# A GEGLU kernel whose head reads its weights on a second DMA queue and computes one tile, not two, the plain way

## The chip, the cores and the metric

The kernel runs on one core of one Trainium2 chip. The metric is the time of one execution in microseconds (us), measured on the device; the number that is quoted is the median of several runs. A profile's span is some 1.8 us shorter than the run's time (273.3 against 275.17 for the kernel before), so spans are compared with spans only.

PE is the matmul engine, DVE VectorE, ACT ScalarE, POOL GpSimd, SP SyncE. SP and ACT each have a DMA queue.

## The reference

```python
B, S, D, F = 32, 32, 1024, 3584        # 1024 tokens, all tensors bf16
def reference(x, w_gate, w_up, w_down):
    return (gelu(x @ w_gate) * (x @ w_up)) @ w_down   # tanh form of gelu
```

## The kernel before

The 3584 features are 28 tiles of 128. The tokens are two halves of 512, and so is the depth of 1024. A tile's gate and up results on both token halves are a 2 by 2 block product, which takes eight half products of four matmuls each. The kernel saves one of the eight with Strassen's scheme in Winograd's form: seven half products, of which P1 = a11·b11 and P2 = a12·b21 use the bf16 inputs as they are, and five use sums of weights (S1 to S4, by POOL) and of x (T1 to T4, by DVE) in fp32r. A tile is then 8 bf16 and 20 fp32r matmuls in place of 32 bf16 ones.

```python
def sums(ci, eng):                       # weights of chunk ci, two tiles each
    a11, a12, a21, a22 = quads(ci)       # gate upper, gate lower, up upper, up lower half of the depth
    yield eng.tensor_tensor(s1, a21, a22, ADD)
    yield eng.tensor_tensor(s2, s1, a11, SUB)
    yield eng.tensor_tensor(s4, a12, s2, SUB)
    yield eng.tensor_tensor(s3, a11, a21, SUB)
```

Sums need x whole and weights of both kinds, and at the start nothing has landed yet. So the head fills the time with work that needs little: tiles 0 and 1 are computed the plain way (32 matmuls each), and P2 of the next ten tiles, which needs only b21 (a quarter of x) and a12 (half of the gate weights), is computed ahead and kept in SBUF. Four tiles of these P2 are called a group here. Group 0's weights are the tile `a12a` (first buffer), group 1's the second buffer of `a12a`, group 2's `a12b`. x arrives as it lies in memory (`x_nat`, transposed by PE) for a first eighth, and by transposing DMAs (`load_xT`) for all else. This is the head's list of loads, in order of issue:

```python
load_nat(nc.sync, 0, 0, HALF)
load_nat(nc.scalar, 0, HALF, NB_P)
...
load_ahead(0, 0, 1)                       # group 0, first of four depth tiles
load_nat(nc.scalar, 1, 0, NB_P)
load_ahead(0, 1, 2, nc.scalar)
for which, eng in enumerate((nc.sync, nc.scalar)):
    load_w(eng, 0, which, KD, KD + KQ)
load_xT(0, KD + KQ, DT)                   # rest of b21, a transposing DMA
load_ahead(0, KQ, KD)                     # rest of group 0
load_w0(nc.sync, KD + KQ, DT)
load_ahead(1, 0, KD)                      # group 1
load_xT(0, 0, KD)                         # b11
load_w0(nc.sync, 0, KD)
load_xT(1, 0, KD)                         # b12
load_xT(1, KD, DT)                        # b22
```

And this is the order of PE's work in the head, with cuts:

```python
# half products of group 0 (depth tiles 0 and 1), as x_nat arrives
plain0(tok0, KD, KD + KQ)                 # tiles 0, 1, first token half
for j, copy in enumerate((nc.scalar.copy, nc.vector.tensor_copy) * 2):
    product_ahead(ps[j], 0, j, KQ)        # rest of group 0; needs the rest of b21
    copy(ahead[0][:, j, :], ps[j])
plain0(tok0, KD + KQ, DT)
...
for j, tag in enumerate("CCAA"):          # group 1
    ...
# tiles 0 and 1, rest of the first token half, then the second half
# P1 of chunk 1, P2 of group 2 (two tiles), then the loop over chunks, from S1·T1 on
```

## Time and profile before

| | before |
|---|---|
| median of 3 runs | 275.38 us (275.07 to 275.65) |
| span of the profiled run | 273.3 us |
| PE busy | 267.9 us, 98% |
| four bf16 matmuls of 512 columns, start to start | 0.86 us, 216 ns each |
| eight fp32r matmuls of 512 columns | 1.81 to 1.84 us, 227 ns each |
| first S1·T1 | 29.18 us |

The page of the kernel before gives, in its parts 1, 3 and 4, the engine's busy time, each DMA queue with its packets, MB and share of 16 engines (q1 is SP's, q10 is ACT's), and the shares of the chain of work that ended last.

```profile
span 273.3 us, 3350 instructions
PE 267.9 (98%) x1190; PEld 188.9 (69%) x1206; DVE 196.6 (72%) x196; ACT 110.8 (41%) x181; POOL 108.3 (40%) x55
...
q1 hardware_dynamic: 50304, 31.00, 39.3%
q10 hardware_dynamic: 3520, 2.56, 2.9%
...
PE 97%; DMA 1%; issue 0%; ACT 0%; SPq 0%
```

PE is nearly all of that chain: nothing else holds the time. SP's queue carries nearly everything. The timeline of PE before, in the head, lists start, length, engine, line, operation with its tiles, count, and in brackets idle time and what ended it. (Tile names come without their numbers: `b` is any quarter of x, `wg` and `wu` are gate and up weights, `t` and `s` the sums.)

```profile
4.45 0.61 PE L285 MATMUL psC<-b,a12a 128*128 128x256 bf16 x2 [0.54 <-DMA a12a<-in_w_gate_dram]
...
6.76 1.03 PE L252 MATMUL psA<-b,wg 128*128 128x512 bf16 x4
7.62 1.03 PE L252 MATMUL psB<-b,wu 128*128 128x512 bf16 x4
...
11.94 1.89 PE L285 MATMUL psC<-b,a12a 128*128 128x512 bf16 x8
13.66 1.89 PE L285 MATMUL psA<-b,a12a 128*128 128x512 bf16 x8
...
29.18 2.12 PE L270 MATMUL psC<-t,s 128*128 128x512 f32 x8
```

There is one piece of idle time, 0.54 us at 4.45 us. After that every start follows the one before by the matmuls' own time: 6.76 to 7.62 is four at 216 ns, 11.94 to 13.66 is eight (1.72 us). The Trainium skill, "TensorE: Matmul & The Clock Gate", Part 1, states about 215.7 ns, and this trace agrees. So there are two ways to a shorter time: fewer matmuls, or less idle head; and the second has little to give.

A table of stretches of the same head gives busy time per engine, granted clock, the share of DMA and, last, GB/s.

```profile
5.00:9.00 4.00, 4.00 (x30) 2.60 (x29) 0.49 (x2) 0.00 (x0) 0.00 (x0) 1.00 1.22 271
9.00:14.00 5.00, 4.95 (x24) 2.27 (x24) 1.52 (x3) 1.75 (x3) 0.00 (x0) 1.00 1.09 277
14.00:20.00 6.00, 6.00 (x30) 2.72 (x28) 3.85 (x4) 4.29 (x5) 0.00 (x0) 1.00 1.07 241
```

The DMA engines moved 271, 277 and 241 GB/s there. They were working all the time, and after 5 us PE never waited for them. Of the issues on SP's queue (start and length of the issuing instruction), these two: group 1's weights, and b11 by a transposing DMA.

```profile
5.44 0.47 SPq L204 DMA_DIRECT2D a12a<-in_w_gate_dram  x1
5.96 4.23 SPq L215 DMA_TRANSPOSE b<-in_x_dram  x1
```

Group 1's weights were issued at 5.44 us, ahead of the b11 transpose. They landed at 10.5 us and were needed at 11.94. The transpose then held SP's sequencer for 4.23 us, so whatever stands behind a transpose on this queue is issued late.

### The profile page before, as it was taken

What the parts mean: (1) busy time and instruction counts of PE and PEld (TensorE: products, weight loads), DVE (VectorE), ACT (ScalarE), POOL (GpSimd) and SP (SyncE); (2) the same over time, 40 slices, a digit from 0 to 9 for tenths busy, and PEclk for the clock granted to TensorE, in tenths of its full rate; (3) what the DMA queues carried; (4) which work ended last, traced back from release to release, by engine and by line L of the source; (5) the groups of instructions that cost most, each with busy time, mean ns of one, the idle gap of its engine ahead of it and who ended that gap; (6) DMA issues with size and microseconds to landing.
All of it is one profiled execution on the core that took longest, in us unless ns stands there. A gap on an engine that the chain in (4) does not pass through costs nothing.

```text
span 273.3 us, 3350 instructions
## 1 busy us (share of the span) xinstructions
PE 267.9 (98%) x1190; PEld 188.9 (69%) x1206; DVE 196.6 (72%) x196; ACT 110.8 (41%) x181; POOL 108.3 (40%) x55
## 2 busy tenths in 40 slices
PE   8999999999999999999999999999999999999995
PEld 4444777877778676676868686754447888888883
DVE  1269996877756676776667576568999999999611
ACT  1271664554643646455563636430300032972001
POOL 1000099997897694949576684000000000000000
PEclk9999999999999999999999999999999999999999
DMA  7994321414505405050514280004992254786202
GB/s 166 290 251 105 111 75 40 117 42 113 156 11 143 137 19 155 0 153 0 156 28 126 79 269 1 0 2 132 329 342 83 93 175 163 240 279 203 78 0 78
DMA packets 53841, 33.77 MB, mean 124 GB/s; under 512 B 9792, under 2 KB 53824, under 8 KB 53824
## 3 DMA queue, kind: packets, MB, share of 16 engines
q1 hardware_dynamic: 50304, 31.00, 39.3%
q10 hardware_dynamic: 3520, 2.56, 2.9%
q8 instruction: 9, 0.15, 0.3%
q14 instruction: 8, 0.07, 0.1%
HBM read 29.62 MB, written 2.10 MB: 116 GB/s over the span
## 4 chain that ended last, share of the span: by engine, by line
PE 97%; DMA 1%; issue 0%; ACT 0%; SPq 0%
PE psA L270 34%; PE psA L446 18%; PE psC L270 17%; PE psC L446 7%; PE psB L446 7%; PE psB L270 5%; PE psB L252 3%; PE psA L252 2%; PE psC L285 2%; PE psA L285 1%; DMA a12a<-in_w_gate_dram 1%; ACT o_sb L586 0%; SPq L191 0%; PE tp L243 0%
## 5 line engine op out<-in xcount | busy, mean ns | idle before, releaser
L270 PE MATMUL psA<-t,s 128*128 128x512 f32 x208 | 54.2, 402 | 0.0
L262 ACT ACTIVATE h<-c 128x512 bf16<-128x512 f32 x52 | 31.6, 627 | 36.6 <-DVE c L350 36.6
L270 PEld LDWEIGHTS psA<-t,s 128*128 128x128 f32 x208 | 39.1, 188 | 9.2
L168 POOL TENSOR_TENSOR s<-wu 128x1024 fp32r<-128x1024 bf16 x12 | 27.4, 2285 | 23.7 <-PE psC L270 12.8
L350 DVE TENSOR_TENSOR c<-sn,psA 128x512 f32<-128x512 f32 x26 | 17.8, 684 | 16.8 <-PE psA L270 16.8
L270 PEld LDWEIGHTS <-wg 128*128 128x128 bf16 x168 | 15.4, 98 | 20.1 <-issue 3.4
L169 POOL TENSOR_TENSOR s<-s,wg 128x1024 fp32r<-128x1024 f32 x12 | 27.7, 2312 | 0.9
L171 POOL TENSOR_TENSOR s<-wg,wu 128x1024 fp32r<-128x1024 bf16 x12 | 26.6, 2216 | 0.0
L355 ACT COPY sn<-psA 128x512 f32<-128x512 f32 x42 | 23.6, 584 | 6.8 <-PE psA L270 6.8
L355 ACT COPY sn<-psC 128x512 f32<-128x512 f32 x26 | 15.2, 588 | 26.9 <-PE psC L270 22.8
L270 PE MATMUL psA<-t,a22r 128*128 128x512 f32 x104 | 25.9, 391 | 0.0
L270 PE MATMUL psC<-t,s 128*128 128x512 f32 x104 | 25.8, 390 | 0.0
L270 PE MATMUL psC<-b22r,s 128*128 128x512 f32 x104 | 25.7, 389 | 0.0
L270 PE MATMUL psA<-b,wg 128*128 128x512 bf16 x100 | 24.1, 379 | 0.2
L270 PEld LDWEIGHTS psC<-t,s 128*128 128x128 f32 x104 | 19.4, 188 | 4.4 <-ACT ahead L377 0.3
L270 PEld LDWEIGHTS psA<-t,a22r 128*128 128x128 f32 x104 | 19.5, 188 | 4.1
L270 PEld LDWEIGHTS psC<-b22r,s 128*128 128x128 f32 x104 | 19.5, 188 | 4.1
L350 DVE TENSOR_TENSOR c<-sn,psC 128x512 f32<-128x512 f32 x26 | 17.7, 688 | 5.5 <-PE psC L270 5.5
L369 DVE TENSOR_TENSOR hi<-h,psA 128x512 bf16<-128x512 bf16 x14 | 9.6, 689 | 12.5 <-PE psA L270 12.5
L425 DVE TENSOR_TENSOR hi<-c,h 128x512 bf16<-128x512 f32 x14 | 18.0, 1284 | 0.5
L425 DVE TENSOR_TENSOR lo<-c,h 128x512 bf16<-128x512 f32 x12 | 17.8, 1479 | 0.6
L170 POOL TENSOR_TENSOR s<-wg,s 128x1024 fp32r<-128x1024 bf16 x8 | 17.3, 2156 | 0.6
(94 smaller groups left out, 396.9 us busy)
## 6 DMA issues: line engine op xcount, KB each, us to landing
wdb<-in_w_down_dram SPq DMA_DIRECT2D x12, 512.0 KB, 5.0
wu<-in_w_up_dram SPq DMA_DIRECT2D x11, 512.0 KB, 4.0
wdb<-in_w_down_dram SPq DMA_DIRECT2D x12, 384.0 KB, 4.7
wg<-in_w_gate_dram SPq DMA_DIRECT2D x6, 512.0 KB, 5.1
wg<-in_w_gate_dram SPq DMA_DIRECT2D x10, 256.0 KB, 4.4
v<-in_w_down_dram SPq DMA_DIRECT2D x4, 512.0 KB, 6.7
out_dram<-o_sb ACTq DMA_DIRECT2D x16, 128.0 KB, 1.7
v<-in_w_down_dram SPq DMA_DIRECT2D x4, 384.0 KB, 7.6
```

The lines of the kernel that those rows point to most:

```text
L168: yield eng.tensor_tensor(s1, a21, a22, ADD)
L169: yield eng.tensor_tensor(s2, s1, a11, SUB)
L170: yield eng.tensor_tensor(s4, a12, s2, SUB)
L171: yield eng.tensor_tensor(s3, a11, a21, SUB)
L252: nc.tensor.matmul(ps, lhsT=w_tiles[0, which][:, dt, fl * P : (fl + 1) * P], rhs=x_rows(dt, nb), start=(dt == first), stop=(dt == last),)
L262: nc.scalar.activation(h, src, ACT.Gelu_apprx_tanh)
L270: nc.tensor.matmul(ps, lhsT=lhs[:, k, :], rhs=rhs[:, k, :], start=(start and k == 0), stop=(k == KD - 1), skip_group_check=True,)
L350: tt(t, s, ps, ADD)
L355: nc.scalar.copy(t, ps)
L369: tt(g_of(ft)[:, :NB], h0, psa, MUL)
L425: tt(g_of(ft)[:, NB:], added(sn5[fl], psa[fl]), h1[fl], MUL)
L446: nc.tensor.matmul(banks[m], lhsT=lhs(k)[:, m * P : (m + 1) * P], rhs=rhs(k), start=(start and k == 0), stop=(k == HF - 1), skip_group_che ...
```

## The change

The change means to save one plain tile's surplus of matmuls. Tile 0 alone is plain; P2 of 16 tiles, not 10, is computed ahead, in four groups. To feed this it puts x's transposes on SP's queue alone, and the weights of the head on ACT's queue, between ACT's copies. T3 = b22 − b12, a DVE operation of 2.28 us, now precedes the two additions that follow P1 of chunk 1. The diff, cut to its core:

```diff
-    NCH = FT // FC
-    NAHEAD = 10
+    chunks = [range(0, 1)] + [range(f0, min(f0 + FC, FT)) for f0 in range(1, FT, FC)]
+    NCH = len(chunks)
+    NAHEAD = 16
...
         load_xT(0, KD + KQ, DT)
-        load_ahead(0, KQ, KD)
-        load_w0(nc.sync, KD + KQ, DT)
-        load_ahead(1, 0, KD)
+        load_ahead(0, KQ, KD, nc.scalar)
+        load_w0(nc.scalar, KD + KQ, DT)
+        load_ahead(1, 0, KD, nc.scalar)
         load_xT(0, 0, KD)
-        load_w0(nc.sync, 0, KD)
         load_xT(1, 0, KD)
         load_xT(1, KD, DT)
+        for which in (1, 0):
+            load_w_all(1, which)
+        load_w_all(2, 0)
...
+        for j in range(KB):
             product_ahead(ps[j], 0, j, KQ)
-            copy(ahead[0][:, j, :], ps[j])
+            both[j % 2](ahead_at[j], ps[j])
+        load_w0(nc.scalar, 0, KD)
+        load_ahead(2, 0, KD, nc.scalar)
+        (plain tile 0, next quarter)
+        group_ahead(1, "CCAA", both)
+        (plain tile 0, rest of the first token half)
+        load_ahead(3, 0, KD, nc.scalar)
+        group_ahead(2, "CCAA")
+        (plain tile 0, second token half; T1, T2, three sums of chunk 1)
+        tt(t3, b22, b12, SUB)
         load_w_all(2, 1)
+        group_ahead(3, "CCAA")
+        nc.scalar.copy(b22r, b22)
...
-        tt(t3, b22, b12, SUB)
         next(chunk1)
```

The lines in parentheses stand for code that is cut. A tile's weights for the plain tile are now rows of 128 columns, 256 bytes, where before they were 256 columns.

More of the change, by code (lines that the diff above doesn't have):

```diff
@@ L74, with g_tile @@
     ps1 = ctx.enter_context(tc.tile_pool(name="ps1", bufs=2, space=bass.MemoryType.PSUM))
+    def g_tile(name, b, dtype=bf16, cols=N):
+        k0, k1 = batches[b]
+        return gpool.tile([P, k1 - k0, cols], dtype, name=name, tag=f"{name[:2]}{k1 - k0}", bufs=2)
     def g_tiles(name, dtype, cols):
-        return [
-            gpool.tile(
-                [P, k1 - k0, cols],
-                dtype,
-                name=name,
-                tag=f"{name[:2]}{k1 - k0}",
-                bufs=2,
-            )
-            for k0, k1 in batches
-        ]
-    g_lo = g_tiles("lo", bf16, N)
+        return [g_tile(name, b, dtype, cols) for b in range(len(batches))]
+    ahead = [gpool.tile([P, KB, NB], fp32, name="ahead", tag=f"lo{KB}", bufs=2)]
+    g_lo = [g_tile("lo", b) for b in range(2)]
+    g_hi = []
     def by_batch(tiles):
@@ L98, in g_of @@
     def g_of(ft):
-        k = ft % HF
-        return by_batch(g_lo if ft < HF else g_hi)(k)
+        k, name, tiles = ft % HF, ("lo", "hi")[ft // HF], (g_lo, g_hi)[ft // HF]
+        if k in (k0 for k0, _ in batches[len(tiles) :]):
+            tiles.append(g_tile(name, len(tiles)))
+        return by_batch(tiles)(k)
     BANKS = {"A": 4, "B": 2, "C": 2}
@@ L117, in x_rows @@
         return ((b11, b12), (b21, b22))[dt // KD][nb][:, dt % KD, :]
-    ahead = [
-        gpool.tile([P, n, NB], fp32, name="ahead", tag=f"hi{n}", bufs=2) for n in (KB, KB, QF - KB)
-    ]
-    assert 2 * KB < NAHEAD <= KB + QF
+    ahead += [gpool.tile([P, n, NB], fp32, name="ahead", tag=f"hi{n}", bufs=2) for n in (KB, QF - KB) * 2]
+    ahead_at = [t[:, k, :] for t in ahead for k in range(t.shape[1])]
+    assert NAHEAD <= len(ahead_at) and NAHEAD % KB == 0
     w_tiles = {}
@@ L131, in load_w @@
     def load_w(eng, ci, which, d0, d1):
-        f0 = ci * FC * P
+        f0, n = chunks[ci][0] * P, len(chunks[ci]) * P
         src = (wg_r, wu_r)[which]
-        eng.dma_start(out=w_tiles[ci, which][:, d0:d1, :], in_=src[:, d0:d1, f0 : f0 + FC * P])
+        eng.dma_start(out=w_tiles[ci, which][:, d0:d1, :n], in_=src[:, d0:d1, f0 : f0 + n])
     def load_w_all(ci, which):
         alloc_w(ci, which)
-        if ci < NCH - 2:
-            load_w(nc.sync, ci, which, 0, KD if which == 0 and is_ahead(ci) else DT)
+        if (ci, which) != (NCH - 1, 0):
+            load_w(nc.sync, ci, which, 0, KD if which == 0 and a12_stays(ci) else DT)
             return
@@ L145, in load_w_all, with a12_stays @@
             load_w(nc.sync, ci, which, d0, d0 + KD)
-    def is_ahead(ci):
-        return 0 < ci and (ci + 1) * FC <= FC + NAHEAD
+    def a12_stays(ci):
+        return 1 <= chunks[ci][0] and chunks[ci][-1] < 1 + 2 * KB
     def quads(ci, fl=None):
-        cols = slice(None) if fl is None else slice(fl * P, (fl + 1) * P)
+        cols = slice(0, len(chunks[ci]) * P) if fl is None else slice(fl * P, (fl + 1) * P)
         wg, wu = w_tiles[ci, 0], w_tiles[ci, 1]
         a12 = wg[:, KD:, cols]
-        if is_ahead(ci):
-            i, j = divmod((ci - 1) * FC, KB)
+        if a12_stays(ci):
+            i, j = divmod(chunks[ci][0] - 1, KB)
             a12 = a12_ahead[i][:, :, j * P : (j + FC) * P][:, :, cols]
@@ L164, in sums @@
         s1, s2, s4, s3 = (
-            spool.tile([P, KD, FC * P], f32r, name=n, tag=n) for n in ("s1", "s2", "s4", "s3")
+            spool.tile([P, KD, FC * P], f32r, name=n, tag=n)[:, :, : len(chunks[ci]) * P]
+            for n in ("s1", "s2", "s4", "s3")
         )
@@ L171, in sums, with chunk_of @@
         yield eng.tensor_tensor(s3, a11, a21, SUB)
+    def chunk_of(ft):
+        ci = next(i for i, c in enumerate(chunks) if ft in c)
+        return ci, ft - chunks[ci][0]
     a22rs = {}
@@ L176, in a22r_of @@
         t = spool.tile([P, KD, P], f32r, name="a22r", tag="a22r", bufs=2)
-        nc.scalar.copy(t, quads(*divmod(ft, FC))[3])
+        nc.scalar.copy(t, quads(*chunk_of(ft))[3])
         a22rs[ft] = t
@@ L202, in load_ahead @@
         def load_ahead(i, k0, k1, eng=nc.sync):
-            f0, n = FC + i * KB, min(KB, NAHEAD - i * KB)
+            f0 = 1 + i * KB
             eng.dma_start(
-                out=a12_ahead[i][:, k0:k1, : n * P],
-                in_=wg_r[:, KD + k0 : KD + k1, f0 * P : (f0 + n) * P],
+                out=a12_ahead[i][:, k0:k1, :],
+                in_=wg_r[:, KD + k0 : KD + k1, f0 * P : (f0 + KB) * P],
             )
@@ L223 @@
             load_w(eng, 0, which, KD, KD + KQ)
+        a12_ahead += [spool.tile([P, KD, KB * P], bf16, name="a12b", tag=t) for t in ("s2", "s4")]
         load_xT(0, KD + KQ, DT)
-        load_ahead(0, KQ, KD)
-        load_w0(nc.sync, KD + KQ, DT)
-        load_ahead(1, 0, KD)
+        load_ahead(0, KQ, KD, nc.scalar)
+        load_w0(nc.scalar, KD + KQ, DT)
+        load_ahead(1, 0, KD, nc.scalar)
         load_xT(0, 0, KD)
-        load_w0(nc.sync, 0, KD)
         load_xT(1, 0, KD)
         load_xT(1, KD, DT)
+        for which in (1, 0):
+            load_w_all(1, which)
+        load_w_all(2, 0)
         warm_ps = acc("A")
@@ L248, with plain @@
         transposed(0)
-        def plain(ps, which, fl, nb, d0, d1, first=0, last=DT - 1):
+        def plain(ps, which, nb, d0, d1, first=0, last=DT - 1):
             for dt in range(d0, d1):
@@ L253, in plain @@
                     ps,
-                    lhsT=w_tiles[0, which][:, dt, fl * P : (fl + 1) * P],
+                    lhsT=w_tiles[0, which][:, dt, :P],
                     rhs=x_rows(dt, nb),
@@ L263, in gelu, with plain_out @@
             return h
-        def plain_out(ft, nb, h, up):
-            tt(g_of(ft)[:, nb * NB : (nb + 1) * NB], h, up, MUL)
+        def plain_out(nb, h, up):
+            tt(g_of(0)[:, nb * NB : (nb + 1) * NB], h, up, MUL)
         def prod(ps, lhs, rhs, start):
@@ L277, in prod @@
                 )
-        def ahead_of(ft):
-            i, j = divmod(ft - FC, KB)
-            return ahead[i][:, j, :]
         def product_ahead(ps, i, j, k0=0, k1=KD, cols=slice(None)):
@@ L292, in product_ahead, with group_ahead @@
                 )
-        ps = [acc(t) for t in "CCAA"]
-        def plain0(tok0, d0, d1):
-            for which in (0, 1):
-                for dt in range(d0, d1):
-                    for fl in range(FC):
-                        plain(tok0[fl][which], which, fl, 0, dt, dt + 1, KD, KD - 1)
+        def group_ahead(i, tags, copies=(nc.scalar.copy,)):
+            for j, tag in enumerate(tags):
+                ps = acc(tag)
+                product_ahead(ps, i, j)
+                copies[j % len(copies)](ahead_at[i * KB + j], ps)
+        ps = [acc(t) for t in "CCAA"]
         for k in range(KQ):
@@ L310 @@
                     transposed(1)
-        tok0 = [(acc("A"), acc("B")) for _ in range(FC)]
-        plain0(tok0, KD, KD + KQ)
-        for j, copy in enumerate((nc.scalar.copy, nc.vector.tensor_copy) * 2):
-            product_ahead(ps[j], 0, j, KQ)
-            copy(ahead[0][:, j, :], ps[j])
-        plain0(tok0, KD + KQ, DT)
-        a12_ahead.append(xpool.tile([P, KD, (NAHEAD - 2 * KB) * P], bf16, name="a12b"))
-        load_w_all(1, 1)
-        load_w_all(1, 0)
-        load_ahead(2, 0, KD)
-        load_w_all(2, 0)
-        for j, tag in enumerate("CCAA"):
-            ps = acc(tag)
-            product_ahead(ps, 1, j)
-            (nc.scalar.copy, nc.vector.tensor_copy)[j % 2](ahead[1][:, j, :], ps)
-        for fl in range(FC):
-            for which in (0, 1):
-                plain(tok0[fl][which], which, fl, 0, 0, KD, KD, KD - 1)
-            plain_out(fl, 0, gelu(tok0[fl][0], "h0", 4), tok0[fl][1])
-            if fl == 0:
-                tt(t1, b12, b11, SUB)
-        tok1 = [(acc("A"), acc("B")) for _ in range(FC)]
-        for fl in range(FC):
-            for which in (0, 1):
-                plain(tok1[fl][which], which, fl, 1, 0, KD)
+        both = (nc.scalar.copy, nc.vector.tensor_copy)
+        tok0 = (acc("A"), acc("B"))
+        for which in (0, 1):
+            plain(tok0[which], which, 0, KD, KD + KQ, KD, KD - 1)
+        for j in range(KB):
+            product_ahead(ps[j], 0, j, KQ)
+            both[j % 2](ahead_at[j], ps[j])
+        load_w0(nc.scalar, 0, KD)
+        load_ahead(2, 0, KD, nc.scalar)
+        for which in (0, 1):
+            plain(tok0[which], which, 0, KD + KQ, DT, KD, KD - 1)
+        group_ahead(1, "CCAA", both)
+        for which in (0, 1):
+            plain(tok0[which], which, 0, 0, KD, KD, KD - 1)
+        plain_out(0, gelu(tok0[0], "h0", 4), tok0[1])
+        load_ahead(3, 0, KD, nc.scalar)
+        group_ahead(2, "CCAA")
+        tt(t1, b12, b11, SUB)
+        tok1 = (acc("A"), acc("B"))
+        for d0 in (0, KD):
+            for which in (0, 1):
+                plain(tok1[which], which, 1, d0, d0 + KD)
+        tok1 = gelu(tok1[0], "h0", 4), tok1[1]
         tt(t2, b22, t1, SUB)
-        nc.scalar.copy(b22r, b22)
         chunk1 = sums(1, nc.vector)
@@ L340 @@
             next(chunk1)
-        for fl in range(FC):
-            for which in (0, 1):
-                plain(tok1[fl][which], which, fl, 1, KD, DT)
-            tok1[fl] = gelu(tok1[fl][0], "h0", 4), tok1[fl][1]
+        tt(t3, b22, b12, SUB)
         load_w_all(2, 1)
+        group_ahead(3, "CCAA")
+        nc.scalar.copy(b22r, b22)
         def added(s, ps):
@@ L360, in first_product @@
                 psa = acc("A")
-                prod(psa, quads(*divmod(ft, FC))[0], b11, True)
-            if ft < FC + NAHEAD:
-                return psa, gelu(added(ahead_of(ft), psa), "h0", 4)
+                prod(psa, quads(*chunk_of(ft))[0], b11, True)
+            if ft <= NAHEAD:
+                return psa, gelu(added(ahead_at[ft - 1], psa), "h0", 4)
             return psa, snap(psa, "sn1")
@@ L373 @@
             prod(p1[fl], quads(1, fl)[0], b11, True)
-        for j, tag in enumerate("CC"):
-            ps = acc(tag)
-            product_ahead(ps, 2, j)
-            nc.scalar.copy(ahead[2][:, j, :], ps)
-        begun = [first_product(FC + fl, p1[fl]) for fl in range(FC)]
-        tt(t3, b22, b12, SUB)
+        begun = [first_product(ft, p1[fl]) for fl, ft in enumerate(chunks[1])]
         next(chunk1)
@@ L383 @@
         nc.gpsimd.tensor_copy(ident[:, :1], t4[:, 0, :1])
-        for fl in range(FC):
-            plain_out(fl, 1, *tok1[fl])
+        plain_out(1, *tok1)
         open_fts = []
         for ci in range(1, NCH):
-            fts = range(ci * FC, (ci + 1) * FC)
-            if fts[0] == HF:
-                g_hi = g_tiles("hi", bf16, N)
+            fts = chunks[ci]
             if ci + 1 < NCH:
@@ L395 @@
                     pass
-            s1, s2, s3, s4 = ([s[:, :, fl * P : (fl + 1) * P] for fl in range(FC)] for s in s_tiles[ci])
+            s1, s2, s3, s4 = ([s[:, :, fl * P : (fl + 1) * P] for fl in range(len(fts))] for s in s_tiles[ci])
             sn5, sn2, h1, h0 = [], [], [], []
@@ L399 @@
             psc = [acc("C") for _ in fts]
-            for fl in range(FC):
+            for fl in range(len(fts)):
                 prod(psc[fl], s1[fl], t1, True)
                 sn5.append(snap(psc[fl], "sn5"))
-            for fl in range(FC):
+            for fl in range(len(fts)):
                 prod(psa[fl], s2[fl], t2, False)
@@ L413 @@
                 load_w_all(ci + 2, 1)
-            if fts[0] < FC + NAHEAD:
+            if fts[-1] <= NAHEAD:
                 h0 = first
             else:
-                for fl in range(FC):
+                for fl in range(len(fts)):
                     psb = acc("B")
@@ L421 @@
                     h0.append(gelu(added(first[fl], psb), "h0", 4))
-            begun = [first_product(ft + FC) for ft in fts] if ci + 1 < NCH else []
+            begun = [first_product(ft) for ft in chunks[ci + 1]] if ci + 1 < NCH else []
             for fl, ft in enumerate(fts):
```

## The prediction

> **What bounds it.** The page gives PE busy 267.9 of 273.3 us, PE 97% of the chain of waits, clock 1.00. The timeline of PE shows one idle piece, 0.54 us at 4.45 us, for the first kept-ahead weights; from 5.2 us on PE streams without a gap. Four bf16 matmuls of 512 columns take 0.86 us there, 216 ns each; the Trainium skill, "TensorE: Matmul & The Clock Gate", Part 1, states about 215.7 ns start to start warm, and the trace agrees. Eight fp32r ones take 1.81 to 1.84 us, 227 ns each. So a chunk of two tiles without P2 (8 bf16, 40 fp32r) is 10.8 us and one with P2 (16, 40) 12.55 by count; the trace has 10.83 and 12.56. Only less PE work or a head stall moves the time.
>
> **Removed, added, moved.** A plain feature tile is 32 bf16 matmuls, 6.91 us; by seven products it is 8 bf16 and 20 fp32r, 6.27 us. One tile moves over: minus 0.64 us (0.23%), all on the critical path. Keeping P2 of 16 tiles ahead instead of 10 moves 24 matmuls (5.2 us) from later chunks to the head. The head then has 6.9 us less plain and 5.2 us more kept-ahead work, so kept-ahead weights are needed sooner, 512 KB each in one transfer. About 1 MB of them is read twice; the queues are under half busy later, so that is free. T3's 2.28 us on DVE move ahead of two adds of 0.69 us; PE had no wait there before (29.4 to 38.5 us is gapless), and DVE still finishes the adds before S2*T2: no change. Chunks of 10.8 us still cover POOL's four sums (8.9 to 9.4 us).
>
> **The head, from issue and landing times.** Unstalled, PE would want group 1's weights at 10.2 us, tile 0's first-half weights at 13.7, group 2's at 15.4, group 3's at 22.3. Before, group 1's were issued at 5.4, landed at 10.5, were needed at 11.9. Now ScalarE waits for earlier transfers whose semaphores it reuses (landings 4.5 to 5.4), so issue is at about 6, while x's transposes, issued from 3.6 on, share the engines: the Trainium skill, "DMA: Bandwidth & Descriptors", "Issuing engines are not separate DMA queues", states that both queues run on the same 16 engines and interleave; no trace here shows a contest yet. Landing 10.8 to 11.4: PE stalls 0.5 to 1.2 us. Group 2's weights are issued after two copies and two other issues, at about 11.5; at the 5 to 6 us that 512 KB took on a full queue they land at 16.5 to 17.5, wanted at about 16.2: another 0 to 1.2. Group 3's and x should be in time. I take 0.8 us of stall as the middle, as my landings may be late.
>
> **Total.** 275.38 - 0.64 + 0.8 = about 275.6 us; range 274.5 to 277.0. Faster by over 2%: 0.01; within 2%: 0.98; slower: 0.01.
>
> **What would show it.** In the timeline PE idle before group 1's first product (releaser: its weights' transfer) and perhaps group 2's; first S1*T1 at 27.5 us plus the stalls, against 29.2; then eight chunks of 10.83 and five of 12.56 us. With no idle the time is 274.7.
>
> **What would make it wrong.** Queue sharing that starves ScalarE's transfers (tile 0's weights late too, over 3 us of stall); ScalarE held by issues so that copies free PSUM banks late; the last chunk, now one tile, exposing latencies of ScalarE and DVE; DVE late for T4 and POOL's first sums.

## The result

The kernel after takes 278.76 us, median of four runs (278.04 to 279.04); the kernel before, on the same chip, takes 275.50, median of four (275.07 to 275.65). The ratio is 1.0117, with a 95% interval of 1.0094 to 1.0140. The direction is clear, the change costs 3.3 us, and that lies outside the range that was predicted. The page of the kernel after has these lines in the parts that were shown of before:

```profile
span 277.1 us, 3357 instructions
PE 268.9 (97%) x1185; PEld 190.7 (69%) x1202; DVE 200.1 (72%) x199; ACT 113.4 (41%) x185; POOL 112.3 (41%) x59
...
q1 hardware_dynamic: 49920, 29.89, 39.5%
q10 hardware_dynamic: 6976, 4.72, 5.9%
...
PE 91%; DMA 6%; issue 0%; SPq 0%; ACT 0%
```

PE's share of the chain has fallen from 97% to 91%, and DMA has 6% of it: PE now waits for transfers. ACT's queue carries 4.72 MB where it carried 2.56. The timeline of PE after shows where (the same columns as before):

```profile
7.35 0.59 PE L262 MATMUL psA<-b,wg 128*128 128x512 bf16 x2
7.78 0.60 PE L262 MATMUL psB<-b,wu 128*128 128x512 bf16 x2
9.86 1.02 PE L291 MATMUL psC<-b,a12a 128*128 128x512 bf16 x4 [1.48 <-DMA b<-in_x_dram]
10.72 1.03 PE L291 MATMUL psA<-b,a12a 128*128 128x512 bf16 x4
12.41 0.61 PE L262 MATMUL psA<-b,wg 128*128 128x512 bf16 x2 [0.66 <-DMA wg<-in_w_gate_dram]
12.85 0.59 PE L262 MATMUL psB<-b,wu 128*128 128x512 bf16 x2
14.24 1.90 PE L291 MATMUL psC<-b,a12a 128*128 128x512 bf16 x7 [0.80 <-DMA a12a<-in_w_gate_dram]
...
18.57 1.03 PE L262 MATMUL psB<-b,wu 128*128 128x512 bf16 x4
19.77 1.90 PE L291 MATMUL psC<-b,a12b 128*128 128x512 bf16 x8 [0.17 <-DMA a12b<-in_w_gate_dram]
...
31.68 2.20 PE L280 MATMUL psC<-t,s 128*128 128x512 f32 x8
```

There are four waits, all for transfers. What each cost is the distance between starts, less the matmuls' own time: 9.86 − 7.78 − 0.43 = 1.65 us for x's first transpose (the idle time shown, 1.48, is shorter, since modelled ends overhang); 12.41 − 10.72 − 0.86 = 0.83 for the gate weights of tile 0; 14.24 − 12.85 − 0.43 = 0.96 for group 1's weights; 19.77 − 18.57 − 0.86 = 0.34 for group 2's. The sum is 3.8 us. Two further terms close the account. The half products of group 0 ended 0.59 us later (first plain matmul at 7.35 us, not 6.76), as the full clock was granted at 6.79 us in this profile and at 5.15 in that of before (and although PE's first wait for group 0's weights, 0.54 us before, is nearly gone). And the counted work is 0.64 us less. 3.8 + 0.6 − 0.6 = 3.8 us, which is the difference of the spans, 277.1 − 273.3.

After 20 us nothing waits. Chunks follow each other at 9.26 us (the first, whose P1 is done before it; 9.18 before), 10.83 (seven intervals), then 12.56 (four) and 11.72, as counted. From the first S1·T1 to the last group of matmuls it is 229.34 us, and 228.11 before: 1.2 us more, where the count has 1.1 more. The last chunk, of one tile, exposed nothing. So the loss is in the head and in nothing else, and the table of stretches after names its place:

```profile
5.00:9.00 4.00, 3.38 (x21) 2.16 (x19) 0.51 (x2) 1.28 (x1) 0.00 (x0) 1.00 1.22 128
9.00:14.00 5.00, 2.92 (x12) 1.08 (x12) 1.38 (x2) 1.17 (x2) 0.00 (x0) 1.00 1.19 256
14.00:20.00 6.00, 5.53 (x25) 2.39 (x27) 1.68 (x3) 3.05 (x4) 0.00 (x0) 1.00 1.24 304
```

From 5 to 9 us the DMA engines moved 128 GB/s, less than half of the 271 of before, while their busy share is the same 1.22. Later they are faster than before, but by then PE has been waiting. The issues on SP's queue, and then those on ACT's, say what was mixed there:

```profile
2.21 14.39 SPq L221 DMA_TRANSPOSE b<-in_x_dram  x4
```

```profile
5.79 0.38 ACTq L210 DMA_DIRECT2D a12a<-in_w_gate_dram  x1
...
14.22 0.39 ACTq L210 DMA_DIRECT2D a12b<-in_w_gate_dram  x1
```

SP spent 14.39 us, from 2.21 on, issuing four transposes one behind the other, while ACT issued the weights into its own queue: group 1's at 5.79. Both kinds were in flight together from 4 to 10 us. The packets show how it went. In the stretch 7 to 8 us before, 386 packets of 512 bytes (median 28 ns) and 111 of 1024 bytes (51 ns) were started; after, it was 181 packets of 256 bytes from SP's queue (18 ns) and 70 of 1024 bytes from ACT's, whose median had grown to 116 ns. x's rest of b21, wanted at about 8.2 us, arrived at 9.8. Neither kind is slow by itself: from 14 to 15 us, when only transposes were moving, the kernel after ran at 290 GB/s,

```profile
14.00:15.00 1.00, 0.76 (x3) 0.41 (x5) 0.00 (x0) 0.00 (x0) 0.00 (x0) 1.00 1.27 290
```

and from 15.5 to 16 us, when only weights in rows of 256 bytes were moving, its packets come to 287 GB/s.

### The profile page after: what moved, and what is told of

Read it like the earlier page. It is cut to its first block, busy times and chain, and to the rows that moved or that the text cites. A ratio compares the mean times of both kernels' runs of the same rounds, so it can differ in the third digit from the quotient of the medians.

```text
span 277.1 us, 3357 instructions
## 1 busy us (share of the span) xinstructions
PE 268.9 (97%) x1185; PEld 190.7 (69%) x1202; DVE 200.1 (72%) x199; ACT 113.4 (41%) x185; POOL 112.3 (41%) x59
## 3 DMA queue, kind: packets, MB, share of 16 engines
q10 hardware_dynamic: 6976, 4.72, 5.9%
## 4 chain that ended last, share of the span: by engine, by line
PE 91%; DMA 6%; issue 0%; SPq 0%; ACT 0%
PE psA L280 35%; PE psA L440 18%; PE psC L280 18%; PE psB L440 7%; PE psC L440 7%; PE psB L280 3%; DMA a12a<-in_w_gate_dram 3%; DMA a12b<-in_w_gate_dram 2%; DMA wg<-in_w_gate_dram 1%; PE psC L291 1%; PE psA L291 1%; PE psA L262 1%; PE psB L262 1%; ACT o_sb L580 0%; SPq L197 0%
## 5 line engine op out<-in xcount | busy, mean ns | idle before, releaser
L280 PE MATMUL psA<-t,s 128*128 128x512 f32 x216 | 56.5, 403 | 0.0
L272 ACT ACTIVATE h<-c 128x512 bf16<-128x512 f32 x54 | 33.0, 628 | 37.8 <-DVE c L352 37.8
L280 PEld LDWEIGHTS psA<-t,s 128*128 128x128 f32 x216 | 40.6, 188 | 9.6
L170 POOL TENSOR_TENSOR s<-wu 128x1024 fp32r<-128x1024 bf16 (+1 forms) x13 | 28.7, 2205 | 22.8 <-DMA wu<-in_w_up_dram 14.7
L171 POOL TENSOR_TENSOR s<-s,wg 128x1024 fp32r<-128x1024 f32 (+1 forms) x13 | 28.6, 2198 | 1.0
L173 POOL TENSOR_TENSOR s<-wg,wu 128x1024 fp32r<-128x1024 bf16 (+1 forms) x13 | 27.8, 2135 | 0.0
L280 PE MATMUL psC<-t,s 128*128 128x512 f32 x108 | 27.0, 391 | 0.0
L280 PEld LDWEIGHTS <-wg 128*128 128x128 bf16 x152 | 13.7, 98 | 18.3 <-issue 3.7
L357 ACT COPY sn<-psA 128x512 f32<-128x512 f32 x38 | 21.4, 586 | 5.9 <-PE psA L280 5.8
L172 POOL TENSOR_TENSOR s<-wg,s 128x1024 fp32r<-128x1024 bf16 (+1 forms) x10 | 20.6, 2056 | 0.8
```

The source lines that it names most:

```text
L272: nc.scalar.activation(h, src, ACT.Gelu_apprx_tanh)
L280: nc.tensor.matmul(ps, lhsT=lhs[:, k, :], rhs=rhs[:, k, :], start=(start and k == 0), stop=(k == KD - 1), skip_group_check=True,)
L357: nc.scalar.copy(t, ps)
```

## The experiments

The first theory is that sharing between the two queues is what starves the head: transposes of SP's queue and copies of ACT's slow each other. Its rivals: the narrow rows of the plain tile's weights are the cause; or the new order of work alone, which wants more bytes sooner, on whatever queue; or T3's new place. Each run below was timed beside the kernel before on the same chip, and ratios are against that.

### e1: the change, with all its weights back on SP's queue

```diff
-        load_ahead(0, KQ, KD, nc.scalar)
-        load_w0(nc.scalar, KD + KQ, DT)
-        load_ahead(1, 0, KD, nc.scalar)
+        load_ahead(0, KQ, KD)
+        load_w0(nc.sync, KD + KQ, DT)
+        load_ahead(1, 0, KD)
         load_xT(0, 0, KD)
+        load_w0(nc.sync, 0, KD)
+        load_ahead(2, 0, KD)
         load_xT(1, 0, KD)
         load_xT(1, KD, DT)
+        load_ahead(3, 0, KD)
...  (and the three later loads on ACT's queue removed)
```

> The changed kernel with every weight load of the head on the SyncE queue again, in the kernel before's order (each transpose of x behind the weights that are wanted sooner). Theory A, two queues: the 3.8 us of PE stalls in the head come from x's long transposes and the weights sharing the transfer engines, which fell to 110 to 140 KB per us between 5 and 9 us. Then here that stretch carries 200 KB per us or more, the stalls shrink to 1 us or less and the time is 274.7 to 276.0 us. Theory B, one plain tile and 16 tiles ahead ask for too many bytes too early whatever the queue: stalls of 2.5 us or more stay, time over 277 us.

It took 278.62 us, ratio 1.0113 (1.0092 to 1.0133): no better than the change. From 5 to 9 us the engines moved 248 GB/s again, and group 1 and tile 0 no longer waited. But the waits turned up later. The timeline of PE in e1 has, besides 0.4 us of short ones, these:

```profile
16.89 1.90 PE L294 MATMUL psC<-b,a12b 128*128 128x512 bf16 x8 [0.80 <-DMA a12b<-in_w_gate_dram]
...
25.17 1.90 PE L294 MATMUL psC<-b,a12b 128*128 128x512 bf16 x8 [1.20 <-DMA a12b<-in_w_gate_dram]
...
33.35 2.14 PE L283 MATMUL psA<-t,s 128*128 128x512 f32 x8 [0.99 <-DVE c L352]
```

The issues on SP's queue in e1 tell why group 3's weights (the second `a12b`) came late, and its table of stretches what the queue brought:

```profile
12.21 6.26 SPq L221 DMA_TRANSPOSE b<-in_x_dram  x2
18.51 0.58 SPq L210 DMA_DIRECT2D a12b<-in_w_gate_dram  x1
```

```profile
9.00:14.00 5.00, 4.95 (x24) 2.09 (x23) 2.08 (x3) 1.85 (x4) 0.00 (x0) 1.00 1.02 199
```

They stood behind two transposes whose issue lasted 6.26 us. The third wait, for DVE's `c`, goes back to a transfer as well: the up weights of chunk 1 held DVE's first sum until 26.75 us (3.20 us of idle DVE). Here is an estimate of what this order of work wants, from the sizes of the loads: x (2.10 MB), tile 0's weights (0.52) and four groups (2.10), 4.7 MB, by 22.3 us, and chunk 1's weights (0.79) some 2 to 3 us later. By 22.3 us the packets of e1 had brought 4.69 MB, parts of later transfers among them, so what was wanted wasn't whole. The packets of the kernel before had brought 5.36 MB by then, and its order wants only 5.2 MB, by some 3 us later. So the new order wants its bytes sooner, its queue brought fewer of them (199 GB/s from 9 to 14 us, in place of 277), and this happens on one queue too. Theory one, as the whole cause, has fallen.

### e2: the kernel before, with only the queue of three loads changed

```diff
-        load_ahead(0, KQ, KD)
-        load_w0(nc.sync, KD + KQ, DT)
-        load_ahead(1, 0, KD)
+        load_ahead(0, KQ, KD, nc.scalar)
+        load_w0(nc.scalar, KD + KQ, DT)
+        load_ahead(1, 0, KD, nc.scalar)
```

> The kernel before with only three groups of weight loads (second half of group 0, second quarter of the plain tiles, group 1) moved to the ScalarE queue, so that x's second transpose is issued at 3.6 us instead of 6. Theory A: transfers fall to 110 to 140 KB per us after 5 us here too, x's first transpose lands at 9 us or later instead of 7.3, PE stalls 1 us or more in the head, and the time is 276.5 to 278.5 us. Theory B: no stall, time within 0.4 us of the kernel before.

It took 278.13 us, ratio 1.0104 (1.0082 to 1.0126). The work and its order are those of the kernel before, and 3 us are lost. Its timeline of PE has two waits, and its table of stretches this line:

```profile
9.86 1.02 PE L285 MATMUL psC<-b,a12a 128*128 128x512 bf16 x4 [1.62 <-DMA b<-in_x_dram]
...
13.38 0.82 PE L252 MATMUL psA<-b,wg 128*128 128x512 bf16 x3 [1.63 <-DMA wg<-in_w_gate_dram]
```

```profile
5.00:9.00 4.00, 3.22 (x21) 1.60 (x18) 0.42 (x2) 1.28 (x1) 0.00 (x0) 1.00 1.23 144
```

It is the picture of the change: b21 in place at 9.86 us, to the hundredth as there, and 144 GB/s in place of 271. So each half of the change was enough by itself to cost about 3 us in these rounds, and the two costs don't add. (That a PE that is late already waits less for the next load would explain this; no run tests it.) The Trainium skill, "DMA: Bandwidth & Descriptors", section "Issuing engines are not separate DMA queues", states that transfers run on the same 16 engines and interleave whoever issues them. This pair of runs agrees, and adds that with transposes on one of the two queues it was not neutral: it lost.

### e3: the change, with b11's transpose held until 6 us

```diff
-        load_xT(0, 0, KD)
-        load_xT(1, 0, KD)
-        load_xT(1, KD, DT)
-        (chunk 1's weights behind them)
...
                 if k == half == 0:
                     transposed(1)
+                    nc.vector.tensor_copy(b11[:, 0, :1], b21[:, 1, :1])
+                    (the same loads, which now wait for this write)
```

> The changed kernel on its two queues, but x's second and later transposes held back by a one-column write of VectorE until about 6 us, as in the kernel before. Theory A1, a second transpose in flight beside the weights of the other queue is what slows both: the first transpose lands at about 7.3 us again, no stall at 8.2 us, total stall 1 to 2 us, time 275.5 to 276.8 us. Theory A2, it is the two queues as such and not the second transpose: the first transpose still lands after 9 us and the time stays over 277.5 us.

It took 278.46 us, ratio 1.0108 (1.0085 to 1.0130). 5 to 9 us moved 150 GB/s, and PE waited 1.78 us at 10.09, now for group 0's weights, and 0.41 and 0.58 later. The rest of b21 still landed at 9.75 us, though the next transpose was issued at 5.95 us and not at 3.60: this is what theory A2 of the expectation forecast, so it is not the early start of the second transpose that makes the first one late. As b21's own transpose still shared the engines with the weights of ACT's queue, the run says nothing more of the mixing.

### e4: the change, with rows of 512 bytes for the plain tile

```diff
-        f0, n = chunks[ci][0] * P, len(chunks[ci]) * P
+        f0, n = chunks[ci][0] * P, (FC if ci == 0 else len(chunks[ci])) * P
```

> The changed kernel with the plain tile's weights fetched 256 columns wide (512 byte rows, twice the bytes, half of them unused) instead of 128 wide (256 byte rows). Theory C: the 256 byte rows of the narrower tile are what slows the transfers in the head; then x's first transpose lands before 8.5 us and the time falls by 1 us or more, below 277.8 us. Theories A and B: no gain, time 278 to 280 us.

It took 279.87 us, ratio 1.0164 (1.0142 to 1.0186). 5 to 9 us moved 230 GB/s and x came in time but for 0.29 us; yet tile 0's and group 1's weights came late, as the lines of PE in e4 show, and then came something new, in the clock column (1.00 elsewhere) of its table of stretches:

```profile
11.83 0.60 PE L262 MATMUL psA<-b,wg 128*128 128x512 bf16 x2 [1.44 <-DMA wg<-in_w_gate_dram]
...
13.89 1.46 PE L291 MATMUL psC<-b,a12a 128*128 128x512 bf16 x3 [1.03 <-DMA a12a<-in_w_gate_dram]
```

```profile
13.00:17.00 4.00, 2.89 (x8) 1.15 (x10) 0.00 (x0) 0.59 (x1) 0.00 (x0) 0.57 1.26 284
```

The record of the granted clock has full speed from 6.45 us, half from 13.28 to 16.69, then full again. The Trainium skill, "TensorE: Matmul & The Clock Gate", Part 1, states windows of 3413 ns whose activity sets the clock; 3.41 us of half clock agree. The window before it, 9.87 to 13.28, had PE busy for about 46% by the timeline. So a head stall can cost twice: here the first eight matmuls of group 1 took 3.10 us from start to start of the next, in place of 1.73. By mean clock, three of e4's four runs had such a window (0.992 to 0.994; 279.69 to 280.31 us) and one had not (1.000; 279.01 us). Narrow rows play some part in the low rate from 5 to 9 us, but e2 had rows of 512 bytes and the low rate as well, so it doesn't need them; and widening them gained nothing, not even in the run at full clock (the change took 278.04 to 279.04).

### e5 and e6: one queue, with the transposes together, and group 3 later

After e1 it was clear that the order on one queue counts. e5 sends all weights up to group 2's ahead of the three large transposes; e6 moves group 3's products behind P1 of chunk 1 as well.

```diff
         load_ahead(1, 0, KD)
-        load_xT(0, 0, KD)
         load_w0(nc.sync, 0, KD)
         load_ahead(2, 0, KD)
+        load_xT(0, 0, KD)
         load_xT(1, 0, KD)
         load_xT(1, KD, DT)
-        load_ahead(3, 0, KD)
         for which in (1, 0):
             load_w_all(1, which)
+        load_ahead(3, 0, KD)
```

(The signs are against e1.) In e6, in addition:

```diff
-        group_ahead(3, "CCAA")
-        nc.scalar.copy(b22r, b22)
...
         for fl in range(FC):
             prod(p1[fl], quads(1, fl)[0], b11, True)
+        group_ahead(3, "CCAA")
+        nc.scalar.copy(b22r, b22)
```

> The one-queue variant with the head's loads in another order: group 1, the plain tile's first half and group 2 first, then x's three large transposes one after the other, then chunk 1's weights, then group 3. Theory D: a transpose that follows weight copies cannot start until all engines have drained them (in the one-queue run 16 first packets waited and ended together at 10.4 us, after 0.24 to 0.69 us), and the rest of that run's 4.4 us of stalls came from the order, group 2 and 3 and chunk 1's weights landing late behind x. One change from copies to transposes instead of three, and weights ahead of x: group 2 and tile 0 without a stall, all stalls 1.5 us or less, time 274.8 to 276.2 us. Theory B, too many bytes too early in any order: still over 277 us.

> The same, and P1 of the first chunk before group 3's products, so that group 3's weights are wanted 1.7 us later and VectorE's two adds can run before T2 is needed. Theory D: at or below the run with the transposes together, by 0 to 1 us; 274.5 to 275.6 us. If the stalls of that run are elsewhere (tile 0's first half), no difference.

e5 took 277.79 us, ratio 1.0089 (1.0047 to 1.0132); e6 277.64, ratio 1.0080 (1.0047 to 1.0113). PE's longer waits in e5:

```profile
15.17 1.02 PE L265 MATMUL psA<-b,wg 128*128 128x512 bf16 x4 [1.02 <-DMA b<-in_x_dram]
...
25.33 1.90 PE L294 MATMUL psC<-b,a12b 128*128 128x512 bf16 x8 [1.37 <-DMA a12b<-in_w_gate_dram]
```

x waits now, as it was put last, and group 3 still does. (A wait of 0.81 us at 4.54 us, for group 0's first weights, comes before these; the kernel before has 0.54 there.) In e6 group 3's wait is gone and x's is 1.09 us, with 0.43 for group 1, 0.19 for chunk 1's gate weights and 0.33 for an ACT copy. A better order recovers about 1 us of the 3.3 by the medians, though the intervals overlap with e1's.

### e7: the change, with plain copies in place of x's transposes

The result is wrong (relative error 1.39): the same bytes of x arrive, not transposed.

```diff
-            nc.sync.dma_start_transpose(
-                out=t[:, d0 % KD : (d1 - 1) % KD + 1, :], in_=xf[nb * NB : (nb + 1) * NB, d0 * P : d1 * P]
-            )
+            nc.sync.dma_start(out=(t, as rows of 1024 or 512 bytes), in_=(the same part of xf))
```

> The changed kernel with x's four transposes replaced by plain copies of the same bytes on the same queue (wrong result on purpose: x is not transposed). Theory A-transpose: it is transposes, not two queues as such, that make the shared engines slow; then 5 to 9 us carries 250 KB per us or more, the stall before group 0's second half is gone, stalls under 1 us in all, time 274.5 to 276 us. Theory A-queues: two queues as such slow each other; then the stretch stays under 180 KB per us and the time over 277 us.

It took 279.92 us, ratio 1.0161 (1.0130 to 1.0192). Its table of stretches, then its longest waits:

```profile
5.00:9.00 4.00, 3.74 (x26) 2.41 (x25) 0.50 (x2) 1.65 (x2) 0.00 (x0) 1.00 1.03 318
```

```profile
13.32 1.90 PE L294 MATMUL psC<-b,a12a 128*128 128x512 bf16 x8 [2.44 <-DMA a12a<-in_w_gate_dram]
...
20.81 1.90 PE L294 MATMUL psC<-b,a12b 128*128 128x512 bf16 x8 [1.64 <-DMA a12b<-in_w_gate_dram]
```

The low rate is gone: 318 GB/s from 5 to 9 us, where transposes on the one queue and copies on the other gave 128, and x came with only 0.26 us of wait. As transposes alone ran at 290 GB/s in the kernel after, the low rate of that stretch belongs to transposes beside copies. (e7 also turns x's packets of 256 bytes into ones of 512 or 1024, so it doesn't part the transposing from the packet size.) But the kernel was slower still. Without transposes to hold SP's sequencer, the rest of x, 1.6 MB that PE didn't want yet, and chunk 1's weights behind it entered SP's queue early and took engine time from ACT's queue, where group 1's and group 2's weights were: 2.44 and 1.64 us of wait. From 5 to 13 us the packets of SP's queue brought 1.7 MB and those of ACT's 0.9. (Three of e7's four runs have a mean clock of 0.992 to 0.994, as in e4, but lie within 0.16 us of the fourth, at 1.000.) The Trainium skill, "DMA: Bandwidth & Descriptors", section "Queues, rings and completion order", states that each engine takes turns between the queues that have work for it, packet by packet. This run agrees as far as it goes: both queues moved data in every microsecond from 5 to 13. A second queue gives away the order of arrival.

### e8: e1 with T3 after the two additions again

```diff
-        tt(t3, b22, b12, SUB)
         load_w_all(2, 1)
...
+        tt(t3, b22, b12, SUB)
         next(chunk1)
```

> The one-queue variant with T3 after the two adds again. In the one-queue run VectorE got chunk 1's weights late (26.75 us) and T3, 2.28 us, stood before the adds that PE waited for (1.0 to 1.25 us of idle at 32.1 us). If T3's place costs there, that idle goes and the time falls by 0.8 to 1.3 us against the one-queue run (278.6), to 277.3 to 277.8 us. If PE then waits for T3 or T4 instead, no change.

It took 277.78 us (276.15 to 278.03), ratio 1.0071 (1.0028 to 1.0113), 0.8 us below e1 by the medians, with overlapping intervals. The profiled run is the one of 276.15. Its longest wait of PE up to 44 us is for POOL's sum in chunk 2, 0.78 us at 37.62, and in e1's place, at 33 us, there is none.

Groups 2 and 3, for which e1's profile shows 0.80 and 1.20 us, did not wait in this run at all, with the same loads in the same order. So one-queue heads of this kind differ by up to 1.9 us from run to run, and one profile of each can't settle what T3's place is worth. In the change itself T3's place caused no wait of PE.

### e9: the best order that was found

From e6: products of group 2's first two tiles ahead of tile 0's, group 3's weights in two transfers, chunk 1's gate weights ahead of its up weights, T3 after the additions, and ACT's copy of b22 ahead of P1 again.

```diff
+        def load_ahead(i, k0, k1, eng=nc.sync, j0=0, j1=KB):
...
-        for which in (1, 0):
+        for which in (0, 1):
             load_w_all(1, which)
-        load_ahead(3, 0, KD)
+        for j in (0, 2):
+            load_ahead(3, 0, KD, j0=j, j1=j + 2)
...
         group_ahead(1, "CCAA", both)
+        group_ahead(2, "CC")
...
-        group_ahead(2, "CCAA")
+        group_ahead(2, "AA", j0=2)
```

> One queue, x's three transposes together, group 2 half before tile 0's first quarter, P1 of chunk 1 before group 3, group 3's weights in two transfers, T3 after the adds again. If the order is all that is left, the stalls shrink to 0.5 us and the first S1*T1 starts at about 27.9 us: 273.3 us of span, 275.0 us, at or below the kernel before. If the bytes bind (by the end of group 3's first half about 5.3 MB are needed; 250 to 262 KB per us were the best so far), PE still waits 1 to 1.5 us for P1's or group 3's weights, first S1*T1 at 28.7 to 29.3, time 275.5 to 276.5 us.

It took 275.72 us, median of six runs (275.19 to 276.08), against 274.99 of the kernel before in the same rounds; ratio 1.0022 (1.0008 to 1.0035). That recovers some 80% of the loss (0.7 of 3.3 us are left by the medians). Of PE's waits, 0.51 us for group 1 is the longest, and the first S1·T1 starts at 28.42 us. But it is still no gain, though its counted work is 0.64 us less: about 1.4 us of short waits, 0.23 of them in chunk 2, eat it up (before has 0.54). From start to start, as above, they come to about 2.3 us against 0.7. No version beat the kernel before.

### e10 and e11: both kernels, with PE's work starting 7 to 8 us later

PE first runs six matmuls of constants, which nobody reads, to raise its clock. With 36 of them its real work starts later, and the transfers have that much more lead.

```diff
-    NWARM = 6
+    NWARM = 36
```

> The kernel before with 30 more warm-up matmuls: PE starts some 6.5 to 7 us later, so every transfer of the head has that much more time. A yardstick for the next run: no stall in the head, 280 to 282 us.

> The changed kernel with the same 30 more warm-up matmuls. If the whole loss is PE waiting for the head's transfers and the counted work is 0.64 us less, the stalls go and this is 0.4 to 0.9 us faster than the kernel before with the same late start (instead of 3.3 us slower without it). If something behind the head costs (T3's place, the last chunk of one tile, 16 tiles ahead), it stays slower.

Before became 281.73 us, ratio 1.0241 (1.0224 to 1.0258), that is 6.7 us more: in its profile PE's first transpose of x came 7.7 us later (11.03 us, not 3.29), and some was won back as the half products now ran at full clock. After became 285.70 (284.09 to 286.91), ratio 1.0391 (1.0366 to 1.0416): 4.0 us behind the other, where it was 3.3 without the delay. But four of its six runs, 285.62 to 286.91, have a mean clock of 0.993 to 0.994, which in e4's profile is one half-clock window (these runs weren't profiled); the two at 0.999 and 1.000 took 284.09 and 284.53, 2.4 and 2.8 us behind e10's median. So at full clock the later start won back some 0.5 to 0.9 of the 3.3 us, an estimate from two runs, and no more. The early waits, for x and for group 1, are gone, but later ones are not; the longest of the profiled run, its fastest:

```profile
22.26 1.04 PE L262 MATMUL psA<-b,wg 128*128 128x512 bf16 x4 [1.04 <-DMA wg<-in_w_gate_dram]
```

Its weights were issued at 16.52 us: they stand between ACT's copies, copies follow PE's products, so the issue moved with PE (it was at 12.38 without the delay) and got no lead over it. And in the meantime, from 14.96 us on, SP's queue had taken up chunk 1's weights, which shared the engines with it. A load that is issued behind copies of PE's products gets no lead from a later start of PE.

### e12 and e13: what the counted work is worth when transfers have lead

e12 is e9 with 36 constants; e13 repeats e10 in the same rounds. With e9's one queue nothing in the head hangs on ACT's copies.

> The best order (one queue) with 30 more warm-up matmuls. No load of its head hangs on a copy of ScalarE, so the later start should give every transfer 6.5 to 7 us more. If the counted work of the change (one plain tile less, 16 tiles ahead) is a gain of 0.5 to 0.64 us once the head is fed, this runs 0.2 to 0.8 us under the kernel before with the same late start (run beside it). If something behind the head costs, it is slower than that by 0.3 us or more.

> The yardstick again, on the same chip and beside the same rounds: 281 to 282.2 us.

e12 took 281.98 us, ratio 1.0236 (1.0216 to 1.0255); e13 took 281.67, ratio 1.0238 (1.0224 to 1.0252). The ratios are equal and the medians 0.3 us apart, so neither forecast is clearly met; but the clock was granted later in e12's profile (5.87 us, and 4.64 in e13's), so its constants took longer. From PE's first transpose of x to its last group of matmuls, first in e12, then in e13:

```profile
11.11 0.39 PE L257 MATMUL tp<-ident,x_nat 128*128 128x128 bf16 x4
...
264.01 6.28 PE L442 MATMUL psA<-tch,hi_r 128*128 128x512 f32 x27
```

```profile
10.52 0.38 PE L243 MATMUL tp<-ident,x_nat 128*128 128x128 bf16 x4
...
263.73 6.51 PE L446 MATMUL psA<-tch,hi_r 128*128 128x512 f32 x28
```

That is 264.01 − 11.11 = 252.90 us and 263.73 − 10.52 = 253.21 (e10 has 253.22): 0.31 us less. In chunk 2 of e12 PE's weight load waited for POOL's sum, and its interval is 11.17 us in place of 10.83, so 0.34 us were lost there. Without that it would be 0.65 less, and the count says 0.64. This is worked out from one profile each, so it supports the count and doesn't prove it by times.

## Why the prediction was wrong

**What bounds it.** Right. PE at 97% of the chain, one idle piece, 216 and 227 ns per matmul: chunks of 10.83 and 12.56 us came as counted, and the later part took 1.2 us more against 1.1 by count.

**Minus 0.64 us for the one tile.** Right, as far as it can be seen: the account of the spans closes with it, and e12 against e13 gives 0.65 after the POOL wait is taken off.

**T3 and POOL: no change.** Right for the change itself: no wait of PE after 20 us. (In one-queue orders, e1 and e8, sums on DVE or POOL did hold PE for 0.99 and 0.78 us.)

**Group 1.** The issue was expected at about 6 us, and was at 5.79. The landing was expected at 10.8 to 11.4, and was at 14.20. The prediction named the sharing but allowed nothing for it: 4.8 to 5.4 us from issue to landing, as the 5.1 us of before. It took 8.4 us, as this transfer shared the engines with transposes and the rate from 5 to 9 us fell to 128 GB/s. That the stall of 0.96 us lies within the 0.5 to 1.2 that was forecast is luck: PE came to it some 2.5 us late, from two waits that were not forecast.

**Group 2.** "Issued after two copies and two other issues, at about 11.5": it was 14.22, 0.02 us after group 1's load landed, whose semaphore it reuses (which semaphore is inferred from these times). The late landing fed on itself. It cost PE only 0.34 us, as PE was late by then.

**"Group 3's and x should be in time."** This is the step that failed most: x's rest of b21 came at 9.8 us and cost 1.65 us, the largest wait of all. The prediction looked at group 1's and 2's transfers, which had changed their queue, and not at the one that stayed in place and now had company. Nor did it forecast a wait for tile 0's second quarter of gate weights, which had changed their queue too: issued at 4.42, they landed at 12.36 and cost 0.83 us. Group 3 was in time.

**"I take 0.8 us of stall as the middle."** The mis-sized term of the sum: it measured 3.8 us. The two stalls that were forecast came to 1.3 us of it (0.96 and 0.34), the two that were not to 2.5 (1.65 and 0.83). With 0.6 us of late clock in the profiled run, which varies from run to run, this is all of the miss: −0.64 + 3.8 is 3.2, and the medians differ by 3.3.

**"What would make it wrong."** "Queue sharing that starves ScalarE's transfers (… over 3 us of stall)" was on that list and is what happened, but it was taken for unlikely and it starved SP's transfers too. What the list didn't have is the second half, which e1 found: the new order of work alone, with no load of the head moved to ACT's queue, already wants its bytes sooner than they come (ratios of 1.0113 in e1 and 1.0071 in e8; one run of e8, at 276.15 us, came within 0.8 us of its rounds' median of before).

**What stays open.** Why transposes and copies in flight together are so slow isn't known; only that the packets take longer. In e1, which has one queue, 18 packets at the start of a large transpose (256 bytes each) began between 9.73 and 10.21 us and all ended at 10.42 to 10.45, taking 240 to 690 ns in place of 18, as if the engines waited for each other; packets don't name their engine in the trace, so that is a guess. The mix is not always slow either: in the kernel after, from 16 to 16.5 us, with a transpose still being issued and weights in rows of 256 bytes beside it, the packets come to 280 GB/s, and at 17 to 19 us, with all transposes issued by 16.6 us, to 354. Why is open; so is why one queue brings less in the new order (e1 against before), for which the narrow rows are one candidate; and what differs in the slower runs of e8.

## What to carry to other kernels

A head in which the engine never waits may still have no slack in its transfers: before moving work forward, add up the bytes that are wanted by each moment and compare them with what the queue has delivered by then. One queue is also an order of arrival; a second queue gives that up, so put on it only what may come late, and look at the transfers that stay as well as at those that move. Don't place the issue of a load behind copies that follow the very engine which the load is to feed.

## What the Trainium skill lacked or had wrong

- "DMA: Bandwidth & Descriptors", "Rules for kernel authors": it says that a transpose next to ordinary transfers needs nothing. No run here gave a wrong result from that. The skill has rates for transposes by themselves, but none for transposes beside ordinary copies: 128 GB/s (the change) and 144 GB/s (e2) from 5 to 9 us, against 271 with the copies ahead of the transpose on one queue and 318 with plain copies on two (e7).
- The same page, "Issuing engines are not separate DMA queues": it calls the time to initiate a transfer usually small beside the transfer. A plain load's issue took mostly 0.4 to 0.6 us here (one of before 1.78), but that of the b11 transpose took 4.23 us before and four transposes took 14.39 us after, and delayed whatever stood behind them on the queue (group 3's weights to 18.51 us in e1).
- "TensorE: Matmul & The Clock Gate", Part 1: it gives half clock after an idle window of about 3.4 us. In e4 the window before the half clock was busy for about 46% (1.56 of 3.41 us, from the timeline), and the longest single idle piece in it was 1.44 us; in e2 two windows in a row that were busy for about 52% by the same count (7.37 to 14.20 us), and in e7 one of 58%, kept the full clock. The page gives 500 ns of variation either way for the first grant, and says that the window runs freely (it also reports 6, 11 or 14 cold matmuls for one kernel, which is wider); here the grant came anywhere from 3.40 (e5) to 6.79 us (the change) in kernels with the same first instructions of PE, a whole window of 3.4 us apart. The 1.64 us between the change's grant and that of before went with half products that ended 0.59 us later.
- No page gives the pace of fp32r matmuls: eight of 512 columns took 1.81 to 1.84 us, 227 ns each, against 216 for bf16.
